# Row maxima of two heads exchanged in full on GpSimd, and one subtracting matrix product per segment part and head, in a causal block attention with a routed feed-forward

## The chip, the cores and the metric

The kernel runs on one core of one Trainium2 chip. The metric is device time in microseconds (us); the kernel before has a median of 488.1 us over 3 runs (486.54 to 491.87).

The engines are called as the profile calls them: PE is TensorE's matrix products and PEld its weight loads (they overlap), DVE is VectorE, ACT is ScalarE, POOL is GpSimd, SP is SyncE, which here only issues DMAs. "L573" is line 573 of the kernel.

## What is computed

q, k and v have shape (8, 8, 576, 64): batch, heads, sequence, head width. The attention is causal over blocks of 64 positions: a query sees its own block of keys and all blocks before it. The result, as 4608 rows of 512, goes through a mixture of eight experts in which each row goes through one of them.

```
scores = scale * np.matmul(q, k.transpose(0, 1, 3, 2))
mask = block_i >= block_j
scores = np.where(mask, scores, -1000000000.0)
scores = scores - np.max(scores, axis=-1, keepdims=True)
attn = np.exp(scores)
attn = attn / (np.sum(attn, axis=-1, keepdims=True) + 1e-09)
attn_out = np.matmul(attn, v)
...
h = np.maximum(x[b, s] @ w1[e], 0.0)
out[b, s] = p[e] * (h @ w2[e])
```

The change touches one step of the attention: the row maximum, and how it is subtracted from the scores before the exponential.

## The kernel before, in words

**Pairs of heads in a pipeline.** The work of the attention is cut into 32 pairs of heads (NPR). One turn of the main loop (L869) works on four pairs at once, each at another stage: pair `a` is loaded, transposed, and its maxima are begun; pair `c = a - 1` gets its scores and exponentials; pair `e = a - 2` is multiplied with v; pair `x = a - 3` is stored and transposed for the gate. The order of instructions on every engine is written out by hand (manual schedule), so each engine works its queue in program order.

**Maxima.** `top` (L507) makes scores with queries on the partitions, in three jobs that share one PSUM buffer (`ps_m`, one copy). Jobs 0 and 1 take the query blocks 4 to 7 and 0 to 1: a product covers two query blocks (128 queries on 128 partitions) for each head, so that after DVE's `reduce_max` (L535) the first 64 partitions of `mx` hold the even block and the last 64 the odd one, with the two heads beside each other in two columns. Job 2 (L526, L543) takes blocks 8, 3 and 2 with a stationary operand in which each half of the partitions belongs to one head; there the halves already hold one head each.

**Exchange before.** After job 1, two copies of 64 x 3 values (L538, on DVE; for pair 0 on ACT) bring into columns 6 to 8 of each half what the other half has of its head. Every block of 4 to 7, 0 and 1 is then found for one head in its own column and for the other in one of the columns 6 to 8. `PLACE` (L505) tells where a block stands.

**Shift.** `shift` (L545) makes on POOL, out of n columns of `mx`, n diagonal blocks of 64 x 64 (`diag`, in bf16; `negi` is minus the identity). It is called for slots 0 to 3 and 4 to 8 after job 1 (L1013 to L1014 for pair 1, L1047 to L1049 for the others, at the end of a turn) and for slots 9 to 11 after job 2 (L889 and L895, at the start of the next turn).

**Scores and the subtraction.** Scores are made transposed, keys on the partitions and queries along the row, in four segments (`SEGS`, L366) of six parts in all: 448 + 64, 256 + 192, 320 and 320 queries. `products` (L550) writes a part for both heads, in fp32. `less` (L558) then adds, with a stationary operand of ones and a moving operand of diagonal blocks, minus the maximum of each query. Blocks 2, 3 and 8 take one product a head (L573). Blocks 0, 1 and 4 to 7 take two for each head (L583), one for the own column and one for the exchanged columns, over every second block. Together these are 34 products a pair (14 of L573, 20 of L583), each with a weight load of the same ones. The two heads use the upper and the lower 64 rows of the array. `expo` (L590) is the exponential on ACT.

**Order around the change.** Within one turn the queues are as follows.

- POOL: `shift` of job 1 from the end of the turn before, then one DMA of feed-forward weights (L64, called at L1062; two of them in turns 4 and 6), then `shift` of job 2 (L895), the cast of the finished rows (L464), three small casts of keys and queries (L976, L978), and the zeroing of a corner of `prob` after each exponential (L598).
- DVE: the reductions of job 1 (L535), the two copies (L538), `norm` of the rows of pair `x` (L481, L482), the reductions of job 2 (L543), the casts of keys and queries (L928, L939), the reduction of job 0 (L535), the small `norm_last` (L489 to L492). In turns 9 to 13, 17 to 21 and 25 to 31 the steps of routing are put between them.
- PE: job 2 of `top` (L526), 8 transposes of pair `a` (L912), 4 transposes of pair `x` (L620) that read what `norm` wrote, single transposes (L631, L963), the products of segments 0 and 1 (L554), `less` for both (L573, L583), job 0 (L515), the outputs of blocks 8 and 6 to 7 (L606, L614), the products and `less` of segments 2 and 3, job 1, and the other outputs (L614).

Of the kernel before, what the change touches and what calls it, by code (L numbers as in the profile page):

```python
# [16 lines left out]
def kernel(  # L17
# [11 lines left out]
    nc = tc.nc  # L29
    F32 = mybir.dt.float32  # L30
    BF16 = mybir.dt.bfloat16
# [4 lines left out]
    ALU = mybir.AluOpType  # L36
# [3 lines left out]
    NB = S // block  # L40
# [5 lines left out]
    P = 128  # L46
# [40 lines left out]
    def rt(shape, dt, name):  # L87
        return rt_p.tile(shape, dt, tag=name, name=name)
# [5 lines left out]
    ones = rt([P, P], BF16, "ones")  # L94
# [37 lines left out]
    scr = rt([P, XGB * XW + XBB * Dm], BF16, "scr")  # L132
# [221 lines left out]
    def slots(inv, tok_g, tok_s):  # L354
# [4 lines left out]
        if tok_s is not None:  # L359
# [6 lines left out]
    SEGS = [[(1, 128, 448, 0), (4, 512, 64, 448)],  # L366
            [(0, 0, 256, 0), (3, 384, 192, 256)],
            [(2, 256, 320, 0)],
            [(0, 256, 320, 0)]]
# [32 lines left out]
    with tc.manual_schedule():  # L402
# [6 lines left out]
        def const(shape, dt, name):  # L409
            return cst.tile(shape, dt, tag=name, name=name)  # L410


        negi = const([P, 64], F32, "negi")
# [14 lines left out]
            nc.gpsimd.memset(vt[i][:, :, :, D:D + 1], 1.0)  # L428
            nc.gpsimd.memset(vt[i][64:128, 4], 0.0)

        diag0 = scr[:, 0:12 * 64].rearrange("p (s t) -> p s t", t=64)
        diag1 = const([P, 12, 64], BF16, "diag")
        nats, pls, mxs, xs, xbs, xTs = {}, {}, {}, {}, {}, {}

        def load_qk(i, engs=(nc.sync,)):
# [59 lines left out]
        def rows(h):  # L495
            return slice(64 * h, 64 * h + 64)
# [8 lines left out]
        PLACE = {4: 0, 6: 2, 0: 4, 2: 9, 3: 10, 8: 11}  # L505

        def top(i, job, pool):  # L507


            ps = pool.tile([P, 2, 512], F32, tag="s" if pool is ps_sp else "m", name="ps_m")  # L510
            flat = ps.rearrange("p b c -> p (b c)")
            if job < 2:
                for k, (b, c, n) in enumerate(PAIRS[job]):
                    for h in range(2):
                        nc.tensor.matmul(ps[:, h, c:c + n], lhsT=qh[rows(h), 64 * b:64 * b + 128],  # L515
                                         rhs=kh[rows(h), 0:n], start=(k == 0), stop=False)
                for h in range(2):
                    last = ps[:, h, :].rearrange("p (k t) -> p k t", t=64)[:, 5 if job else 7:8:2, :]
                    nc.tensor.matmul(last, lhsT=unseen[rows(h), :],  # L519
                                     rhs=ones[rows(h), :].rearrange("p (k t) -> p k t", t=64)  # L520
                                     [:, 0:2 if job else 1, :], start=False, stop=True)
                return ps
            for (b, c, n) in FULL:
                for (k0, nn) in ((0, min(n, 512)), (512, n - 512)):
                    if nn > 0:
                        nc.tensor.matmul(flat[:, c + k0:c + k0 + nn], lhsT=qd[:, PLACE[b] - 9, :],  # L526
                                         rhs=kh[:, k0:k0 + nn], start=True, stop=True)
            return ps

        def maxima(i, job, ps):  # L530
            flat = ps.rearrange("p b c -> p (b c)")
            mx = mxs[i]
            if job < 2:
                for (b, c, n) in PAIRS[job]:
                    nc.vector.reduce_max(mx[:, PLACE[b]:PLACE[b] + 2], ps[:, :, c:c + n], axis=AX)  # L535
                if job == 1:
                    for h in range(2):
                        (nc.vector.tensor_copy if i else nc.scalar.copy)(  # L538
                            mx[rows(h), 6:9], mx[rows(1 - h), h:6:2])
                return  # L540
            for (b, c, n) in FULL:
                z = PLACE[b]
                nc.vector.reduce_max(mx[:, z:z + 1], flat[:, c:c + n], axis=AX)  # L543

        def shift(i, s0, n):  # L545
            nc.gpsimd.tensor_tensor(  # L546
                (diag1 if i else diag0)[:, s0:s0 + n, :], negi[:, None, :].to_broadcast([P, n, 64]),
                mxs[i][:, s0:s0 + n, None].to_broadcast([P, n, 64]), op=ALU.mult)

        def products(i, ps, s, part):  # L550

            j, a, n, c = SEGS[s][part]
            for h in range(2):
                nc.tensor.matmul(ps[:, h, c:c + n],  # L554
                                 lhsT=pls[i][rows(h), S + 128 * j:S + 128 * j + 128],
                                 rhs=pls[i][rows(h), a:a + n], start=part == 0, stop=False)

        def less(i, ps, s, part):  # L558

            j, a, n, c = SEGS[s][part]  # L560
            diag = diag1 if i else diag0
            blocks = range(a // 64, (a + n) // 64)
            ends = part == len(SEGS[s]) - 1
            for b, w in ((0, 1), (2, 2), (4, 2), (8, 1)):
                if b not in blocks:
                    if b == 4 and 6 in blocks:
                        b, w = 6, 1
                    else:
                        continue
                o, z = c + 64 * b - a, PLACE[b]  # L570
                if b in (2, 8):
                    for h in range(2):
                        nc.tensor.matmul(ps[:, h, o:o + 64 * w], lhsT=ones[rows(h), :],  # L573
                                         rhs=diag[rows(h), z:z + w, :], start=False,
                                         stop=ends and b + w - 1 == blocks[-1])
                    continue
                for e in range(2):
                    for h in range(2):
                        out_s = ps[:, h, o:o + 128 * w].rearrange("p (m e t) -> p m e t", e=2, t=64)
                        zz = slice(z + h, z + h + 2 * w - 1, 2)  # L580
                        if e:
                            zz = slice(6 + z // 2, 6 + z // 2 + w)
                        nc.tensor.matmul(out_s[:, :, e ^ h, :], lhsT=ones[rows(h), :],  # L583
                                         rhs=diag[rows(h), zz, :], start=False,
                                         stop=ends and e == 1 and b + 2 * w - 1 == blocks[-1])

        def seg_tile():
            return ps_sp.tile([P, 2, 512], F32, tag="s", name="ps_s")
# [280 lines left out]
        for it in range(-2, NPR):  # L869
            a, c, e, x = it + 2, it + 1, it, it - 1  # L870
# [14 lines left out]
                last_ps = top(c, 2, ps_mp) if c > 1 else second  # L885
            if last_ps is not None and not on_a:
                maxima(c, 2, last_ps)
                shift(c, 9, 3)
            if on_x:  # L889
                norm(x, g0_b, 0, 6)  # L890
            run(it, "top")
            run(it, "begin", ge)
            if last_ps is not None and on_a:
                maxima(c, 2, last_ps)
                shift(c, 9, 3)  # L895
            if on_x:
                store_x(x, nc.gpsimd.tensor_copy if it < NPR - 1 else nc.scalar.copy)
            if it == NPR - 1:
# [2 lines left out]
            if on_a:  # L901
# [3 lines left out]
                else:  # L905
                    ps = ps_sp.tile([P, 2, 512], F32, tag="s", name="ps_t")
# [84 lines left out]
            if on_c:  # L991
                ps0, ps1 = seg_tile() if c else opened, seg_tile()
                if c:
                    products(c, ps0, 0, 0)
                products(c, ps1, 1, 0)
                products(c, ps1, 1, 1)
                if c:
                    products(c, ps0, 0, 1)
                else:
                    maxima(a, 0, top(a, 0, ps_mp))  # L1000
                if a in (1, 2):
                    g1 = turns()
                if a == 1:
                    load_weights(halves.pop(0))
                for z, ps in enumerate((ps0, ps1)):
                    less(c, ps, z, 0)
                    less(c, ps, z, 1)
                    expo(c, ps, z)
# [2 lines left out]

            if a == 1:
                maxima(a, 1, top(a, 1, ps_mp))  # L1013
                shift(a, 0, 4)  # L1014
                shift(a, 4, 5)
            elif on_a:
                maxima(a, 0, top(a, 0, ps_mp))
            if on_x and not on_a:
# [16 lines left out]
            if on_c:  # L1035
                pss = seg_tile(), seg_tile()
                products(c, pss[0], 2, 0)
                products(c, pss[1], 3, 0)
                if a == 1:
                    second = top(a, 2, ps_mp)  # L1040
                for z in range(2):
                    less(c, pss[z], z + 2, 0)
                    expo(c, pss[z], z + 2)
            run(it, "late", g1)
            if on_a:
                if a != 1:
                    maxima(a, 1, top(a, 1, ps_mp if a else ps_sp))  # L1047
                    shift(a, 0, 4)
                    shift(a, 4, 5)  # L1049
                if a == 0:  # L1050

                    opened = seg_tile()
                    products(a, opened, 0, 0)
                    products(a, opened, 0, 1)
                    maxima(a, 2, top(a, 2, ps_mp))
                    shift(a, 9, 3)
            if it >= 0:

                for _ in range(2 if it in (4, 6) else 1):
# [179 lines left out]
```

## Time and profile before

| what | value |
|---|---|
| median of the runs | 488.1 us (486.54 to 491.87, 3 runs) |
| profiled execution, device time | 487.98 us |
| its span, first to last instruction | 486.2 us |
| mean granted TensorE clock | 0.993 |
| instructions in the span | 19978 |
| POOL busy | 267.5 us (55%) |
| ACT busy | 252.3 us (52%) |
| HBM | 170 GB/s over the span |

The profile is of one execution. Its device time is 1.8 us longer than its span, and it lies 0.1 us below the median. A busy share is an average over all stages: the attention loop runs until about 335 us, the feed-forward after it. In the timeline, a row gives the start, the time from the first start to the last end of the instructions merged in it, engine, line, operation, tiles, count, and in brackets the idle time before it with what ended it.

### The profile page before, as it was taken

What the parts mean: (1) busy time and instruction counts of PE and PEld (TensorE: products, weight loads), DVE (VectorE), ACT (ScalarE), POOL (GpSimd) and SP (SyncE); (2) the same over time, 40 slices, a digit from 0 to 9 for tenths busy, and PEclk for the clock granted to TensorE, in tenths of its full rate; (3) what the DMA queues carried; (4) which work ended last, traced back from release to release, by engine and by line L of the source; (5) the groups of instructions that cost most, each with busy time, mean ns of one, the idle gap of its engine ahead of it and who ended that gap; (6) DMA issues with size and microseconds to landing.
All of it is one profiled execution on the core that took longest, in us unless ns stands there. A gap on an engine that the chain in (4) does not pass through costs nothing.

```text
span 486.2 us, 19978 instructions
## 1 busy us (share of the span) xinstructions
PE 469.7 (97%) x7959; PEld 374.7 (77%) x7980; DVE 343.4 (71%) x868; ACT 252.3 (52%) x512; POOL 267.5 (55%) x477
## 2 busy tenths in 40 slices
PE   8999999999999999999999999999999999999992
PEld 6687888888878888887888887878777777676770
DVE  5688767778898887889877879996468953434330
ACT  4645555455545455554555554544545545555551
POOL 3455444544445554444554345354587778888761
PEclk9999999999999999999999999999999999999997
DMA  7787999997999789787888878634556666667541
GB/s 153 137 179 135 167 171 185 187 158 148 172 165 157 149 156 170 147 162 145 138 164 161 166 142 165 104 60 100 122 152 149 132 151 164 145 150 150 149 115 50
DMA packets 180974, 71.33 MB, mean 147 GB/s; under 512 B 165008, under 2 KB 173200, under 8 KB 180880
## 3 DMA queue, kind: packets, MB, share of 16 engines
q1 hardware_dynamic: 161920, 37.93, 38.4%
q0 software_dynamic: 17760, 31.79, 35.1%
q8 instruction: 66, 1.08, 1.0%
q10 hardware_dynamic: 1200, 0.30, 0.3%
q14 instruction: 28, 0.23, 0.2%
HBM read 67.45 MB, written 14.97 MB: 170 GB/s over the span
## 4 chain that ended last, share of the span: by engine, by line
PE 86%; DVE 6%; DMA 2%; issue 2%; POOL 1%; ACT 1%; POOLq 0%; DVEq 0%; ACTq 0%
PE ps_s L554 18%; PE g L614 15%; PE ps_h L744 13%; PE ps_o L756 12%; PE ps_t L912 5%; PE g L606 4%; PE ps_m L526 3%; PE g L620 3%; PE ps_s L583 3%; PE ps_m L515 3%; DMA out_dram<-o_sb,tok2s 2%; DVE mx L535 2%; PE g L663 2%; PE ps_s L573 2%; DVE mx L543 1%
## 5 line engine op out<-in xcount | busy, mean ns | idle before, releaser
L593 ACT ACTIVATE prob<-ps_s 128x640 f32<-128x640 f32 (+2 forms) x128 | 100.2, 834 | 86.7 <-PE ps_s L573 62.7
L554 PE MATMUL ps_s<-plb 64*128 64x320 f32 (+4 forms) x768 | 105.9, 407 | 0.0
L535 DVE TENSOR_REDUCE mx<-ps_m 128x2 f32<-128x1024 f32 (+2 forms) x96 | 80.2, 864 | 32.3 <-PE ps_m L519 32.1
L546 POOL TENSOR_TENSOR diag<-negi,mx 128x256 bf16<-128x256 f32 (+2 forms) x93 | 59.5, 640 | 52.8 <-DVE mx L535 18.1
L614 PE MATMUL g<-vt,prob 128*64 128x65 f32 x2560 | 87.7, 223 | 0.2 <-issue 0.2
L554 PEld LDWEIGHTS ps_s<-plb 64*128 64x128 f32 x768 | 66.8, 186 | 24.8 <-issue 9.6
L598 POOL MEMSET prob<- 64x128 f32 x128 | 23.9, 200 | 108.5 <-ACT prob L593 108.5
L614 PEld LDWEIGHTS g<-vt,prob 128*64 128x64 f32 x2560 | 80.3, 138 | 3.7 <-issue 0.3
L756 PE MATMUL ps_o<-w_bf,hT 128*128 x283 | 67.4, 379 | 1.7 <-issue 0.7
L748 ACT ACTIVATE hT<-ps_h 128x512 bf16<-128x512 f32 x76 | 45.2, 597 | 19.8 <-PE ps_h L744 19.5
L924 ACT COPY plb<-ps_t 128x512 f32<-128x512 f32 x58 | 31.1, 589 | 42.5 <-PE ps_t L912 42.5
L760 ACT ACTIVATE o_sb<-ps_o,share 128x512 f32<-128x512 f32 x38 | 26.1, 687 | 45.8 <-PE ps_o L756 39.8
L756 PEld LDWEIGHTS <-hT 128*128 128x128 bf16 x304 | 28.3, 98 | 27.8
L543 DVE TENSOR_REDUCE mx<-ps_m 128x1 f32<-128x576 f32 (+2 forms) x96 | 43.0, 503 | 3.8 <-PE ps_m L526 3.6
L720 DVE COPY natb<-w_bf 128x4096 bf16 x20 | 24.6, 1228 | 29.9 <-PE ps_h L744 27.4
L720 DVE COPY plb<-w_bf 128x4096 bf16 x20 | 24.5, 1227 | 26.5 <-PE ps_h L744 25.3
L744 PEld LDWEIGHTS <-natb 128*128 128x128 bf16 x608 | 35.5, 98 | 4.6 <-issue 0.3
L744 PEld LDWEIGHTS <-plb 128*128 128x128 bf16 x608 | 35.5, 98 | 4.4 <-issue 0.3
L766 POOL DMA_INDIRECT out_dram<-o_sb,tok x20 | 30.3, 1517 | 13.2 <-ACT o_sb L760 8.2
L766 POOL DMA_INDIRECT out_dram<-o_sb,tok2s x18 | 30.7, 1704 | 11.6 <-ACTq L1191 4.8
L912 PE MATMUL ps_t<-id_f,natb 128*128 128x128 f32 x232 | 30.1, 273 | 0.0
L583 PEld LDWEIGHTS <-ones 64*128 64x128 bf16 x640 | 23.4, 94 | 7.8 <-issue 5.4
(271 smaller groups left out, 827.6 us busy)
## 6 DMA issues: line engine op xcount, KB each, us to landing
w_bf<-in_moe_w_dram POOLq DMA_DIRECT2D x32, 512.0 KB, 6.5
vt<-in_v_dram SPq DMA_DIRECT2D x64, 128.0 KB, 4.0
natb<-in_k_dram SPq DMA_DIRECT2D x63, 128.0 KB, 4.0
natb<-in_q_dram SPq DMA_DIRECT2D x63, 128.0 KB, 3.4
x_rows<-xb SPq DMA_DIRECT2D x32, 128.0 KB, 5.4
natb<-in_k_dram SPq DMA_DIRECT2D x32, 32.0 KB, 2.5
vt<-in_v_dram SPq DMA_DIRECT2D x32, 32.0 KB, 6.5
x_rows<-xb SPq DMA_DIRECT2D x64, 8.0 KB, 3.9
```

What stands on the lines that cost most here:

```text
L535: nc.vector.reduce_max(mx[:, PLACE[b]:PLACE[b] + 2], ps[:, :, c:c + n], axis=AX)
L543: nc.vector.reduce_max(mx[:, z:z + 1], flat[:, c:c + n], axis=AX)
L546: nc.gpsimd.tensor_tensor((diag1 if i else diag0)[:, s0:s0 + n, :], negi[:, None, :].to_broadcast([P, n, 64]), mxs[i][:, s0:s0 + n, None]. ...
L554: nc.tensor.matmul(ps[:, h, c:c + n], lhsT=pls[i][rows(h), S + 128 * j:S + 128 * j + 128], rhs=pls[i][rows(h), a:a + n], start=part == 0, ...
L593: nc.scalar.activation(p[:, :, SEG0[s]:SEG0[s] + w], ps[:, :, 0:w], func=AF.Exp, scale=scale_attn)
L614: nc.tensor.matmul(g[rows(e), o + 65 * h:o + 65 * h + 65], lhsT=p[:, h, c:c + 64], rhs=t[:, j, h, :], start=(j == 0), stop=(j == m))
L720: nc.vector.tensor_copy(w, w1_bf[:, bass.ds(off, WE)])
L744: nc.tensor.matmul(ps_h[:, f, :], lhsT=w[:, ko * F + fo * P:ko * F + fo * P + P], rhs=xb[:, ko * P:(ko + 1) * P], start=(ko == 0), stop=(k ...
L748: nc.scalar.activation(hT[:, half * 4:half * 4 + 4, :], ps_h, func=AF.Relu)
L756: nc.tensor.matmul(ps_o, lhsT=hT[:, fo, :], rhs=w2_bf[:, bass.ds(woff + fo * Dm, Dm)], start=(fo == 0), stop=(fo == FO - 1))
L766: wr = nc.gpsimd.indirect_dma_start(out=out_flat, out_offset=bass.IndirectOffsetOnAxis(ap=g[1][:, g[3]:g[3] + 1], axis=0), in_=o_sb, in_of ...
L912: tr = nc.tensor.transpose(pw[w][:, 128 * t:128 * t + 128], nat[:, 4 * w + t].rearrange("p h d -> p (h d)"), id_f)
```

## The change

The exchange becomes a full one. Three copies of 64 x 3 values, on POOL (for pair 0 on ACT), swap the odd columns of the first half with the even columns of the second, with columns 6 to 8 of the second half as the place in between. After that each half holds one head for all blocks. `shift` is now called by block instead of by slot, so `diag` has 9 blocks instead of 12 in the order of the queries: blocks 4 to 7 and then 0 to 1 after job 1, blocks 2 to 3 and then 8 after job 2. `less` is one product for each part and head, over all its blocks.

```
-        diag0 = scr[:, 0:12 * 64].rearrange("p (s t) -> p s t", t=64)
-        diag1 = const([P, 12, 64], BF16, "diag")
+        diag0 = scr[:, 0:NB * 64].rearrange("p (s t) -> p s t", t=64)
+        diag1 = const([P, NB, 64], BF16, "diag")
...
                 if job == 1:
-                    for h in range(2):
-                        (nc.vector.tensor_copy if i else nc.scalar.copy)(
-                            mx[rows(h), 6:9], mx[rows(1 - h), h:6:2])
+                    copy = nc.gpsimd.tensor_copy if i else nc.scalar.copy
+                    copy(mx[rows(1), 6:9], mx[rows(0), 1:6:2])
+                    copy(mx[rows(0), 1:6:2], mx[rows(1), 0:6:2])
+                    copy(mx[rows(1), 0:6:2], mx[rows(1), 6:9])
...
-        def shift(i, s0, n):
+        def shift(i, b, n):
+            z = PLACE[b]
             nc.gpsimd.tensor_tensor(
-                (diag1 if i else diag0)[:, s0:s0 + n, :], negi[:, None, :].to_broadcast([P, n, 64]),
-                mxs[i][:, s0:s0 + n, None].to_broadcast([P, n, 64]), op=ALU.mult)
+                (diag1 if i else diag0)[:, b:b + n, :], negi[:, None, :].to_broadcast([P, n, 64]),
+                mxs[i][:, z:z + n, None].to_broadcast([P, n, 64]), op=ALU.mult)
...
             j, a, n, c = SEGS[s][part]
             diag = diag1 if i else diag0
...
+            for h in range(2):
+                nc.tensor.matmul(ps[:, h, c:c + n], lhsT=ones[rows(h), :],
+                                 rhs=diag[rows(h), a // 64:(a + n) // 64, :], start=False,
+                                 stop=part == len(SEGS[s]) - 1)
...
                 maxima(c, 2, last_ps)
-                shift(c, 9, 3)
+                shift(c, 2, 2)
+                shift(c, 8, 1)
...
                 maxima(a, 1, top(a, 1, ps_mp))
-                shift(a, 0, 4)
-                shift(a, 4, 5)
+                shift(a, 4, 4)
+                shift(a, 0, 2)
```

The last two hunks stand for all places: `shift(c, 9, 3)` occurs in three places (L888, L895 and, for pair 0, L1056), the pair of `shift(a, 0, 4)` and `shift(a, 4, 5)` in two. The two branches of `less` by block are gone.

More of the change, by code (lines that the diff above doesn't have):

```diff
@@ L561, in less @@
             diag = diag1 if i else diag0
[L562 to L585, printed above, removed]
+            for h in range(2):
+                nc.tensor.matmul(ps[:, h, c:c + n], lhsT=ones[rows(h), :],
+                                 rhs=diag[rows(h), a // 64:(a + n) // 64, :], start=False,
+                                 stop=part == len(SEGS[s]) - 1)
         def seg_tile():
@@ L894 @@
                 maxima(c, 2, last_ps)
-                shift(c, 9, 3)
+                shift(c, 2, 2)
+                shift(c, 8, 1)
             if on_x:
@@ L1047 @@
                     maxima(a, 1, top(a, 1, ps_mp if a else ps_sp))
-                    shift(a, 0, 4)
-                    shift(a, 4, 5)
+                    shift(a, 4, 4)
+                    shift(a, 0, 2)
                 if a == 0:
@@ L1055 @@
                     maxima(a, 2, top(a, 2, ps_mp))
-                    shift(a, 9, 3)
+                    shift(a, 2, 2)
+                    shift(a, 8, 1)
             if it >= 0:
```

## Prediction

> **What bounds the kernel now.** I read the totals and the chain of work that ended last first, to learn which engine a saving must come from; then one plain turn in order of time; then the waits of PE.
>
> ```profile
> PE 469.7 (97%) x7959; PEld 374.7 (77%) x7980; DVE 343.4 (71%) x868; ACT 252.3 (52%) x512; POOL 267.5 (55%) x477
> ...
> PE 86%; DVE 6%; DMA 2%; issue 2%; POOL 1%; ACT 1%; POOLq 0%; DVEq 0%; ACTq 0%
> ```
>
> PE carries 86% of the chain, DVE 6%, POOL 1%. A busy PE counts pipelined products at full latency, so 97% isn't yet "at its peak"; what matters is the step from one start to the next. The chain shows these steps, in a plain turn (168.2 to 178.0 us):
>
> ```profile
> 172.49 0.06 PE ps_s L573 x2
> ...
> 172.92 0.22 PE ps_m L515 x2
> ...
> 176.11 0.11 PE ps_s L583 x4
> ...
> 176.39 0.22 PE ps_m L515 x4
> ```
>
> The 22 products of `less` for segments 0 and 1 occupy PE from 172.49 to 172.92, 0.43 us; the 12 for segments 2 and 3 from 176.11 to 176.39, 0.28 us. L515 streams 512 columns a head in 0.22 us, both heads at once: 0.43 ns a column. `less` moves 960 columns a head in the first group and 640 in the second, at that rate 0.41 and 0.27 us. So the small products already run at the speed of their columns.
>
> The same turn in order of time shows who waits:
>
> ```profile
> 167.82 0.58 PE L614 MATMUL g<-vt,prob 128*64 128x65 f32 x14
> ...
> 167.99 0.61 POOL L546 TENSOR_TENSOR diag<-negi,mx 128x256 bf16<-128x256 f32 x1 [0.50 <-DVE mx L535]
> ...
> 168.21 0.59 DVE L538 COPY mx<-mx 64x3 f32<-64x3 f32 x2
> ...
> 168.78 1.04 PE L912 MATMUL ps_t<-id_f,natb 128*128 128x128 f32 x8
> 168.83 0.20 DVE L481 RECIPROCAL rs<-g 128x6 f32<-128x6 f32 x1
> 168.95 0.72 POOL L546 TENSOR_TENSOR diag<-negi,mx 128x320 bf16<-128x320 f32 x1 [0.34 <-PE ps_m L526]
> 169.06 0.56 DVE L482 TENSOR_TENSOR x<-g,rs 128x384 f32<-128x384 f32 x1
> ...
> 169.54 1.34 DVE L543 TENSOR_REDUCE mx<-ps_m 128x1 f32<-128x576 f32 x3
> 169.61 0.74 POOL L64 DMA_DIRECT2D w_bf<-in_moe_w_dram  x1
> ...
> 169.77 0.63 PE L620 MATMUL g<-id_f,x 128*128 128x128 f32 x4
> ...
> 170.80 0.42 DVE L928 CAST kh<-plb 128x512 bf16<-128x512 f32 x1
> ...
> 171.04 0.54 POOL L546 TENSOR_TENSOR diag<-negi,mx 128x192 bf16<-128x192 f32 x1 [0.69 <-DMA vt<-in_v_dram]
> ...
> 172.33 0.22 PE L573 MATMUL ps_s<-diag,ones 64*128 64x128 bf16 x2
> ```
>
> Read it from the copies. DVE ends them at 168.80 and only then begins `norm` (168.83 to 169.62). PE's transposes L620 read `norm`'s result and begin at 169.77. POOL's last diagonal blocks are ready at 171.58, `less` needs them at 172.33: 0.75 us of room. POOL is idle between 170.35 and 171.04, because it waits for DVE's L543 (ends 170.88). In a turn where `norm` was early, the same two PE rows are:
>
> ```profile
> 66.16 1.04 PE L912 MATMUL ps_t<-id_f,natb 128*128 128x128 f32 x8
> ...
> 67.03 0.60 PE L620 MATMUL g<-id_f,x 128*128 128x128 f32 x4
> ```
>
> From the first L912 to the first L620 there it is 0.87 us, in the plain turn 0.99, and L620 itself takes 0.63 instead of 0.60. So PE loses 0.15 us a plain turn behind DVE's copies. The view of waits counts such turns:
>
> ```profile
> PEld g L620 <- issue: 2.3, 14, 0.2
> ...
> PE ps_m L526 <- DVE mx L535: 1.6, 3, 0.6
> ```
>
> The first row is the gap ahead of L620, 14 times. The second is three turns in which routing fills DVE and PE waits over half a microsecond for the reductions of job 1; there DVE is the chain for a whole turn.
>
> **The change part by part.**
>
> *Products of `less`.* 34 become 12 a pair, 1088 become 384, with as many fewer weight loads; the columns stay the same. Gain: 0.43 - 0.41 and 0.28 - 0.27, 0.03 us a pair, over 32 pairs 0.9 us. Bounds: nothing, and twice that from the rounding of the chain's rows. I take 0.9.
>
> The Trainium skill ("TensorE: Matmul & The Clock Gate", Back-to-back issue gap) gives a sustained pace of about 81 ns a product at 128 columns, set by product and weight load together. Thirty-four of them at that pace would be 2.8 us a pair, where this trace has 0.71; the measurement decides, and the rule's direction (many small products are dear) is the first rival.
>
> *Copies off DVE.* `norm` can then start when PE's outputs are there. L614 of the turn before ends at 168.40; the shortest step from such an output to a DVE reader is read here:
>
> ```profile
> 173.73 1.10 PE L614 MATMUL g<-vt,prob 128*64 128x65 f32 x32
> ...
> 174.95 0.18 DVE L489 RECIPROCAL rs<-g 128x3 f32<-128x3 f32 x1 [0.52 <-PE g L614]
> ```
>
> It is 0.12 us, so `norm` starts at 168.52 instead of 168.83, 0.31 us earlier, and ends at 169.31. That is before PE comes to L620 (169.65), so the whole 0.15 us go, 14 times: 2.1 us. What is late next is PE itself. In the three DVE-bound turns the same 0.31 us come off the wait of 0.55: 0.9 us in all. Bounds of these two together: nothing (another wait takes over), and 2.1 + 1.6 = 3.7. I take 3.0.
>
> *Three copies onto POOL.* No row shows a POOL copy of 64 x 3. The nearest are small and simple:
>
> ```profile
> L598 POOL MEMSET prob<- 64x128 f32 x128 | 23.9, 200 | 108.5 <-ACT prob L593 108.5
> ...
> L976 POOL CAST kh<-plb 128x64 bf16<-128x64 f32 x32 | 7.6, 238 | 7.2 <-ACT plb L974 7.2
> ...
> L538 DVE COPY mx<-mx 64x3 f32<-64x3 f32 x62 | 18.1, 291 | 1.5
> ```
>
> Below, 0.20 each, 0.6 for three back to back. Each copy reads or overwrites what the one before touched, on other partitions, so it may wait for its end. For a step between two dependent POOL instructions I have only the start of the kernel, where the identity is set to zero and then filled:
>
> ```profile
> 0.81 0.20 POOL masks.py:197 MEMSET id_f<- 128x128 f32 x1 [0.29 <-POOLq L1223]
> ...
> 1.16 0.28 POOL masks.py:199 TENSOR_SCALAR_AFFINE_SELECT id_f<-id_f 128x128 f32<-128x128 f32 x1
> ```
>
> From end to start 0.15. Above, DVE's mean of 0.29 plus 0.15, three times: 1.33 us. I take 0.9, three times 0.2 plus two waits of 0.15, as a copy of 3 columns is nearer to the small rows.
>
> The Trainium skill ("GPSIMD Engine Reference", Instruction dispatch) states that consecutive Pool instructions are no barrier between its cores and that a reader of another core's partitions needs a wait; this speaks for the waits in that sum, and no row here shows these copies.
>
> *Shift.* By the rows of L546 256 elements take 0.61, 320 take 0.72, 192 take 0.54: some 0.1 for each 64. So 128 take 0.41 and 64 take 0.30 (estimates). After job 1, 0.61 + 0.72 become 0.61 + 0.41; after job 2, 0.54 becomes 0.71 in two instructions. POOL's queue in the plain turn is then: reductions end 168.17, first copy 168.33 (DVE to POOL is 0.16 at 170.88 to 171.04), copies to 169.23, blocks 4 to 7 to 169.84, 0 to 1 to 170.25, weight DMA to 170.99. DVE's L543 now ends at 170.57, so POOL is no longer idle but the later one: blocks 2 to 3 and 8 are ready at 171.70. `less`, 0.15 earlier, needs them by 172.18 - 0.05. Hidden, with 0.43 us of room instead of 0.75. Behind POOL's queue stand the cast L464, its DMAs on SP, and L976 and L978, all 0.1 to 0.2 later; their readers are the next turn's loads and job 2, microseconds away. If the cover goes, PE waits directly (rival three).
>
> DVE's casts run just then and can hold POOL up. One such row:
>
> ```profile
> 202.38 1.02 POOL L546 TENSOR_TENSOR diag<-negi,mx 128x192 bf16<-128x192 f32 x1 [0.94 <-DMA vt<-in_v_dram]
> ```
>
> 1.02 instead of 0.54: 0.48 lost. With one such loss the blocks are ready at 172.18, 0.05 too late; I count that at nothing here.
>
> *Where POOL isn't hidden: the last pair.* At 322.9 there is no next pair and nothing between job 2 and `less`:
>
> ```profile
> 322.96 0.59 DVE L538 COPY mx<-mx 64x3 f32<-64x3 f32 x2
> ...
> 323.70 0.72 POOL L546 TENSOR_TENSOR diag<-negi,mx 128x320 bf16<-128x320 f32 x1 [0.34 <-PE ps_m L526]
> ...
> 324.36 0.79 POOL L64 DMA_DIRECT2D w_bf<-in_moe_w_dram  x1
> ...
> 325.24 0.49 POOL L546 TENSOR_TENSOR diag<-negi,mx 128x192 bf16<-128x192 f32 x1
> ...
> 325.79 0.23 PE L573 MATMUL ps_s<-diag,ones 64*128 64x128 bf16 x2 [0.22 <-POOL diag L546]
> ```
>
> Here PE waits for POOL already. New: copies from 323.09 to 323.99, shifts to 325.01, DMA to 325.80, two shifts to 326.51, `less` at 326.56: 0.8 us later. Turns 4 and 6 have a second weight DMA of 0.74 ahead of the shift and may lose 0.1 each.
>
> *Pair 0.* ACT makes three copies instead of two, ahead of a cast that is on the chain:
>
> ```profile
> 10.05 0.40 ACT L538 COPY mx<-mx 64x3 f32<-64x3 f32 x2 [2.03 <-DVE mx L535]
> ...
> 10.47 0.59 ACT L932 CAST kh<-g 128x512 bf16<-128x512 f32 x1
> ```
>
> 0.20 more.
>
> *Sum.* -0.9 - 3.0 + 0.8 + 0.2 + 0.2 = -2.7 us. The profiled execution took 487.98 us, so 485.3; it stands 0.1 below the median of the runs, which I leave out.
>
> **The rivals.**
>
> *Weight loads were the price.* The loads of ones are busy for 45.9 us:
>
> ```profile
> L573 PEld LDWEIGHTS <-ones 64*128 64x128 bf16 x448 | 22.5, 102 | 0.6 <-issue 0.3
> ...
> L583 PEld LDWEIGHTS <-ones 64*128 64x128 bf16 x640 | 23.4, 94 | 7.8 <-issue 5.4
> ```
>
> Were PE held by them, 704 of 1088 gone would be 29.7 us: 458. Against it: 22 products in 0.43 us, 20 ns each, while a load takes 94; they overlap. Chance 0.04.
>
> *The wait moves and nothing is gained.* L620 no longer waits, but PE then waits elsewhere for as long (for DVE's casts, for ACT), and the three DVE-bound turns stay. Left are -0.9 + 1.2: 488.3. Against it: PE's waits within the loop in the view of waits are these two rows and gaps of 0.1 to 0.2 that recur whoever was last. Chance 0.18.
>
> *Slower: POOL's chain outlasts its room in every turn.* Place: the product of blocks 8 in front of `less`. Copies at 1.33 us end at 169.66, the weight DMA at 171.42, the two shifts at 172.13, with one loss of 0.48 at 172.61; `less` begins at 172.66, 0.33 later than before, in some 28 turns: +9.2; gains of `norm` are then worth nothing, `less` gives 0.9, last pair (0.4 dearer), turns 4 and 6 and pair 0 cost 1.6. Sum 488.0 + 9.9 = 497.9. It decides from 172.28 on (before's start less 0.05), and passes 1% at 0.18 us a turn more. For it: POOL's reserve shrinks in any case. Against: before, POOL lost its 0.48 in only a few turns. Chance 0.14.
>
> The Trainium skill ("SBUF — State Buffer", SBUF: two separate sides) says that GpSimd and a DVE instruction in a two-port mode take a shared port as an exclusive lock for a whole instruction. The 1.02 above agrees with it; two shifts in place of one could be held twice.
>
> **How the numbers follow.** Forecast 485.3 with a chance of 0.64, its own range 483.4 (both waits gone, `less` at twice its gain, copies at 0.6: -4.6) to 487.5 (half of the 3.0 lost, and POOL 0.05 too late in 14 turns: +2.2). The rivals have 0.04, 0.18 and 0.14. The range, 482.3 to 491.0, takes in the second rival and the mild part of the third, and leaves out the first and most of the third; below, it goes 1.1 further than the forecast's own, since the runs of before alone differ by more (486.54 to 491.87). About 1%, 4.9 us, is what a measurement of this kernel can tell from no change: faster than 483.1 has 0.04 from the first rival and 0.06 from the forecast's tail; slower than 493.0 has 0.12 from the third; within has 0.78.
>
> **What would show it.** Right: 12 rows of `less` a pair, the chain's steps at 0.41 and 0.27 us; L481 about 0.3 us after the reductions' end instead of behind copies; the row of L620's gap gone; L526's wait for L535 at about 0.2 us; POOL's wait for L543 gone in plain turns. Wrong: a row in which PE waits for L546 in more than a handful of turns (third rival); L554 or L515 with new waits of 0.15 (second); `less` far below 0.41 us (first).

## The result, and the profile after

The changed kernel takes 484.87 us (median of 7 runs, 484.32 to 485.98). Its ratio to the kernel before is 0.9924, with a 95% interval of 0.9896 to 0.9953: 0.8% faster. Its profiled execution took 484.87 us, with a span of 483.2. The forecast was 485.3.

The totals and the chain of work that ended last:

```profile
PE 468.3 (97%) x7276; PEld 369.1 (76%) x7276; DVE 327.1 (68%) x806; ACT 252.4 (52%) x513; POOL 271.6 (56%) x602
...
PE 75%; POOL 9%; issue 7%; DMA 4%; DVE 2%; POOLq 1%; ACT 0%; DVEq 0%
```

PE has 683 products fewer on record and yet only 1.4 us less busy time. DVE lost 16 us. The chain's share of POOL (9%, it was 1%) comes from the gathers of the feed-forward, not from the attention: within the loop the chain runs almost wholly over PE, from turn to turn. In its steps, in a plain turn:

```profile
170.50 0.41 PE ps_s L568 x8
170.91 0.22 PE ps_m L515 x2
...
174.10 0.27 PE ps_s L568 x4
174.37 0.22 PE ps_m L515 x4
```

`less` is L568 now. Eight products take 0.41 us where 22 took 0.43, four take 0.27 where twelve took 0.28. The same turn in order of time:

```profile
166.39 0.18 POOL L540 COPY mx<-mx 64x3 f32<-64x3 f32 x1 [0.74 <-DVE mx L535]
...
166.60 0.20 DVE L481 RECIPROCAL rs<-g 128x6 f32<-128x6 f32 x1 [0.27 <-PE g L599]
166.64 0.18 POOL L541 COPY mx<-mx 64x3 f32<-64x3 f32 x1
...
166.83 0.56 DVE L482 TENSOR_TENSOR x<-g,rs 128x384 f32<-128x384 f32 x1
...
166.88 0.18 POOL L542 COPY mx<-mx 64x3 f32<-64x3 f32 x1
166.93 1.04 PE L899 MATMUL ps_t<-id_f,natb 128*128 128x128 f32 x8
167.15 0.97 POOL L551 TENSOR_TENSOR diag<-negi,mx 128x256 bf16<-128x256 f32 x2
...
167.81 0.60 PE L605 MATMUL g<-id_f,x 128*128 128x128 f32 x4
168.06 0.74 POOL L64 DMA_DIRECT2D w_bf<-in_moe_w_dram  x1
...
168.82 0.89 POOL L551 TENSOR_TENSOR diag<-negi,mx 128x128 bf16<-128x128 f32 x2
...
170.33 0.58 PE L568 MATMUL ps_s<-diag,ones 64*128 64x448 bf16 x8
```

DVE's `norm` (L481) now waits for PE's outputs, 0.27 us after the reductions, and no longer stands behind copies. It ends at 167.39, and PE goes from the transposes L899 to L605 in 0.88 us (166.93 to 167.81) without a gap; L605 takes 0.60 instead of 0.63. POOL's last blocks are ready at 169.71, 0.62 us ahead of `less`.

In the routing turns that DVE set, PE now starts L526 nearly in step:

```profile
134.63 1.28 DVE L535 TENSOR_REDUCE mx<-ps_m 128x2 f32<-128x768 f32 x2
...
135.95 0.20 DVE L481 RECIPROCAL rs<-g 128x6 f32<-128x6 f32 x1
...
136.05 0.60 PE L526 MATMUL ps_m<-kh,qd 128*128 128x512 bf16 x4 [0.15 <-PE g L599]
```

Its gap was 0.55 and is 0.15. DVE still sets these turns: L526 starts 0.14 us after the reductions L535 end (135.91), as it did before (0.15). Measured from one start of L526 to the next, by the chain and the timeline, the turns are as follows; turns in which `norm` was early anyway are mostly 0.03 shorter.

| turn | before | after |
|---|---|---|
| plain (45.02 to 54.84; 45.59 to 55.23) | 9.82 | 9.64 |
| set by DVE (209.58 to 219.93; 207.33 to 217.17) | 10.35 | 9.84 |

From the second start of L526 to the last the loop shrank from 307.67 us (15.41 to 323.08) to 302.72 (16.37 to 319.09), by 4.95. The span shrank by 3.0; the difference was lost at both ends.

At the start, the inputs of this execution came later, which the change doesn't touch: DVE's first reduction begins at 8.28, before at 7.59. What is the change's own is the third copy on ACT:

```profile
10.73 0.19 ACT L540 COPY mx<-mx 64x3 f32<-64x3 f32 x1 [1.61 <-DVE mx L535]
10.96 0.19 ACT L541 COPY mx<-mx 64x3 f32<-64x3 f32 x1
11.19 0.19 ACT L542 COPY mx<-mx 64x3 f32<-64x3 f32 x1
...
11.40 0.58 ACT L919 CAST kh<-g 128x512 bf16<-128x512 f32 x1
```

The cast on the chain starts 0.67 after the first copy; before it was 0.42 (10.05 to 10.47). At the end, the last pair:

```profile
319.00 0.18 POOL L540 COPY mx<-mx 64x3 f32<-64x3 f32 x1 [0.74 <-DVE mx L535]
...
319.75 0.97 POOL L551 TENSOR_TENSOR diag<-negi,mx 128x256 bf16<-128x256 f32 x2
...
320.67 0.79 POOL L64 DMA_DIRECT2D w_bf<-in_moe_w_dram  x1
...
321.48 0.81 POOL L551 TENSOR_TENSOR diag<-negi,mx 128x128 bf16<-128x128 f32 x2
...
322.35 0.59 PE L568 MATMUL ps_s<-diag,ones 64*128 64x448 bf16 x8 [0.77 <-POOL diag L551]
```

From the last start of L526 (319.09) to `less` it is 3.26 us; before it was 2.71 (323.08 to 325.79). PE waits 0.77 for POOL there, and this is the only wait of PE for L551 in the loop.

### The profile page after: what moved, and what is told of

The parts are those of the page before. It is cut to its first block, busy times and chain, and to the rows that moved or that the text cites. A ratio compares the mean times of both kernels' runs of the same rounds, so it can differ in the third digit from the quotient of the medians.

```text
span 483.2 us, 18592 instructions
## 1 busy us (share of the span) xinstructions
PE 468.3 (97%) x7276; PEld 369.1 (76%) x7276; DVE 327.1 (68%) x806; ACT 252.4 (52%) x513; POOL 271.6 (56%) x602
## 4 chain that ended last, share of the span: by engine, by line
PE 75%; POOL 9%; issue 7%; DMA 4%; DVE 2%; POOLq 1%; ACT 0%; DVEq 0%
PE ps_s L559 20%; PE g L599 16%; PE ps_t L899 5%; PE ps_h L729 5%; PE ps_o L741 5%; PE g L591 5%; PE ps_s L568 5%; POOL scr L689 4%; PE ps_m L526 3%; POOL xg L689 3%; PE ps_m L515 3%; PE g L605 3%; DMA out_dram<-o_sb,tok2s 2%; POOL out_dram L751 2%; PE g L648 2%
## 5 line engine op out<-in xcount | busy, mean ns | idle before, releaser
L535 DVE TENSOR_REDUCE mx<-ps_m 128x2 f32<-128x1024 f32 (+2 forms) x96 | 80.3, 864 | 35.4 <-PE ps_m L519 33.8
L599 PEld LDWEIGHTS g<-vt,prob 128*64 128x64 f32 x2560 | 80.1, 138 | 3.3
L741 PE MATMUL ps_o<-w_bf,hT 128*128 x304 | 71.5, 379 | 0.1
L551 POOL TENSOR_TENSOR diag<-negi,mx 128x256 bf16<-128x256 f32 (+1 forms) x124 | 58.6, 491 | 9.9 <-DVE mx L546 5.2
L751 POOL DMA_INDIRECT out_dram<-o_sb,tok x20 | 24.6, 1232 | 16.1 <-ACT o_sb L745 12.6
L568 PE MATMUL ps_s<-diag,ones 64*128 64x448 bf16 (+1 forms) x372 | 31.5, 274 | 0.8 <-POOL diag L551 0.8
L899 PE MATMUL ps_t<-id_f,natb 128*128 128x128 f32 x232 | 30.1, 273 | 0.0
L591 PEld LDWEIGHTS g<-vt,prob 128*64 128x64 f32 x640 | 21.3, 137 | 7.2 <-issue 6.2
```

Source lines behind the costliest of these rows:

```text
L551: nc.gpsimd.tensor_tensor((diag1 if i else diag0)[:, b:b + n, :], negi[:, None, :].to_broadcast([P, n, 64]), mxs[i][:, z:z + n, None].to_b ...
L568: nc.tensor.matmul(ps[:, h, c:c + n], lhsT=ones[rows(h), :], rhs=diag[rows(h), a // 64:(a + n) // 64, :], start=False, stop=part == len(SE ...
L591: nc.tensor.matmul(g[rows(h), 130:195], lhsT=p[:, h, c:c + 64], rhs=t[:, j, h, :], start=(j == 0), stop=(j == 4))
L599: nc.tensor.matmul(g[rows(e), o + 65 * h:o + 65 * h + 65], lhsT=p[:, h, c:c + 64], rhs=t[:, j, h, :], start=(j == 0), stop=(j == m))
L741: nc.tensor.matmul(ps_o, lhsT=hT[:, fo, :], rhs=w2_bf[:, bass.ds(woff + fo * Dm, Dm)], start=(fo == 0), stop=(fo == FO - 1))
L899: tr = nc.tensor.transpose(pw[w][:, 128 * t:128 * t + 128], nat[:, 4 * w + t].rearrange("p h d -> p (h d)"), id_f)
```

## The experiments

The theory: the gain is the copies' time off DVE's queue, which lets `norm` start earlier; the products give only their 0.03 us a pair; POOL takes the copies for nothing because it has room. The rivals: the fewer products and weight loads are the gain; or POOL is already what a turn waits for.

The experiments ran in three sessions, each on a chip of its own: e1 to e4 in the first, e5_act_last_dma, e6 and e7 in the second, the runs named "again" and e8 in the third. There the kernel before takes 498.2 to 498.7 us, and single runs spread over several us. In the changed kernel the difference lies behind the loop: from the last start of L526 to the end it takes 175.0 us in the third session and 164.1 in the result. So totals are given as ratios to the kernel before in the same session, and the verdicts rest on the turns of the loop, which repeat to 0.01 us where nothing disturbs them (9.64 for a plain turn of the changed kernel, there and in the result).

**The changed kernel again** (a0_after_again, no edit).

> The changed kernel again, unedited, beside the edits below on one chip. If the gain is the loop's 0.17 a plain turn and 0.5 in three turns, the ratio to the kernel before is again 0.992 to 0.995, whatever the chip's own time is.

Ratio 0.9945 (0.9908 to 0.9982), as expected. Plain turns 9.64, DVE's turns 9.85.

**Old exchange, its two copies on POOL** (e1_pool_copies).

```
-                        (nc.vector.tensor_copy if i else nc.scalar.copy)(
+                        (nc.gpsimd.tensor_copy if i else nc.scalar.copy)(
```

> The kernel before with one edit: the two copies of the old exchange run on GpSimd instead of VectorE; the 34 products of less stay. Theory (the gain comes from taking the copies off VectorE's queue ahead of norm): the gap ahead of L620 goes and the three VectorE-bound turns get 0.5 shorter, so 485.5, 0.8 above the changed kernel, which is what the products give. Rival (the gain is the fewer products and weight loads): 487.5 to 488.5.

```profile
44.46 0.61 PE L526 MATMUL ps_m<-kh,qd 128*128 128x512 bf16 x4
...
54.13 0.61 PE L526 MATMUL ps_m<-kh,qd 128*128 128x512 bf16 x4
```

A plain turn takes 9.67 us: of the 0.18 that the change gives, 0.15 come with this edit alone, with all 34 products still there. The turns set by DVE take 9.95 instead of 10.35. The total doesn't follow: ratio 0.9986 (0.9960 to 1.0013), where 485.5 of 488.1, so 0.995, was expected; it lies where the rival had it. The turns speak against the rival, since the gain in them is there without fewer products. Its profile, of an execution of 500.5 us where the median is 497.7, shows where time went instead, in stretches where PE waits for nothing that the profile shows:

```profile
PE g L614 <- issue: 2.1, 3, 1.3
PE ps_s L554 <- issue: 2.0, 1, 2.0
```

Over the loop its turns are some 7 us longer than others of their kind. In the changed kernel's first profile this view has one such stretch in the loop, of 0.2. More of this below.

**Full exchange, on DVE** (e2_exchange_dve).

```
-                    copy = nc.gpsimd.tensor_copy if i else nc.scalar.copy
+                    copy = nc.vector.tensor_copy if i else nc.scalar.copy
```

> The changed kernel with the full exchange on VectorE: three copies instead of two ahead of norm, 12 products a pair. Theory: VectorE's copies take 0.6 to 0.9 a turn where they took 0.59, norm starts 0 to 0.3 later than in the kernel before, less gives 0.8: 487.2 to 491. Rival (fewer products and weight loads are the gain): 484.9, as the changed kernel.

```profile
45.78 0.54 PE ps_m L526 x4
...
55.53 0.54 PE ps_m L526 x4
```

A plain turn takes 9.75 to 9.76, DVE's turns 10.21; ratio 0.9995 (0.9970 to 1.0019). With the 12 products but the exchange on DVE, most of the gain is gone. By their turns, the rival of the products falls on this and the run before. In the totals neither half of the change alone can be told from the kernel before (0.9986 and 0.9995), and only both together can. DVE's copies were cheaper than I had allowed:

```profile
167.85 0.16 DVE L540 COPY mx<-mx 64x3 f32<-64x3 f32 x1
...
168.24 0.17 DVE L542 COPY mx<-mx 64x3 f32<-64x3 f32 x1
...
168.44 0.20 DVE L481 RECIPROCAL rs<-g 128x6 f32<-128x6 f32 x1
```

Three take 0.16 each. Of the two of before the first took 0.42 and the second 0.16, in nearly every turn: the first ran beside POOL's shift and ended with it (168.63, the shift at 168.60), the second came after it. Now POOL waits for the copies.

**One product for each block** (e3_less_by_block, and again as e3_again).

```
-            for h in range(2):
-                nc.tensor.matmul(ps[:, h, c:c + n], lhsT=ones[rows(h), :],
-                                 rhs=diag[rows(h), a // 64:(a + n) // 64, :], start=False,
-                                 stop=part == len(SEGS[s]) - 1)
+            for b in range(a // 64, (a + n) // 64):
+                o = c + 64 * b - a
+                for h in range(2):
+                    nc.tensor.matmul(ps[:, h, o:o + 64], lhsT=ones[rows(h), :],
+                                     rhs=diag[rows(h), b, :], start=False,
+                                     stop=part == len(SEGS[s]) - 1 and 64 * b + 64 == a + n)
```

> The changed kernel with less cut into one product for each block of 64 queries and head: 50 products and weight loads a pair instead of 12, the same columns. Theory (columns set the time, some 2 ns more for each pair of products): 44 ns a pair of heads, 1.4 us in all: 486.3, and the chain's rows of less at about 0.46 and 0.29 us. Rival (a weight load costs the 42 ns of the rival's price): 1216 more loads, 51 us, about 536.

> 50 products a pair again, beside the changed kernel. Theory of the columns alone: 1.4 us above the changed kernel. Rival (TensorE also stands without a wait shown when its instruction stream is longer, 7 us in the first profile of this kernel, 0.2 in the changed one): 4 to 8 us above it.

```profile
39.70 0.44 PE ps_s L570 x30
40.13 0.22 PE ps_m L515 x2
...
43.32 0.29 PE ps_s L570 x20
43.61 0.22 PE ps_m L515 x4
```

Fifty products take 0.44 and 0.29 us where twelve take 0.41 and 0.27; a plain turn is 9.69, 0.05 longer. So 38 more products with their weight loads cost 0.05 us, about 1.3 ns each, and the price of 42 ns is refuted. But the totals rise by more than the 1.4 us that this makes over 27 turns: ratios 1.0020 (0.9989 to 1.0050) and 1.0036 (1.0002 to 1.0069), the second beside 0.9945 for the changed kernel in the same session, 4.5 us by the ratios. In the second profile the loop is 306.47 us against 302.34: 1.4 from the products, and the rest from a few turns that are 0.4 to 0.8 too long. One of them in the chain:

```profile
84.97 0.56 issue
85.53 0.34 PE g L601 x4
```

PE stands in the middle of a run of equal products. The kernel before stands in the same turn, four products before the same L526, and once more two turns later:

```profile
85.29 0.17 issue
...
105.51 0.29 issue
```

The changed kernel doesn't there, in any session. It stands at another place, ahead of the gate's products (L648) in the turn that starts at 136 us in the result, which is 0.25 longer than its kind there. PE stands at the same place with one more POOL instruction (e6), with the last DMA moved (e8) and with the copies on ACT as well (e5_again), all with 12 products:

```profile
148.12 0.43 PE L648 MATMUL g<-xT,wgl 128*32 128x128 f32 x8 [1.23 <-issue]
146.70 0.43 PE L648 MATMUL g<-xT,wgl 128*32 128x128 f32 x8 [0.88 <-issue]
146.58 0.43 PE L648 MATMUL g<-xT,wgl 128*32 128x128 f32 x8 [0.60 <-issue]
```

The traces show what these places have in common. The thirteen profiles have 27 such stands of over 0.15 us in the loop. If PE's products and weight loads are counted from the start of the trace, each stand comes after a number of them that leaves 193 when it is divided by 256, so the stands of a trace lie whole blocks of 256 instructions apart. And each time a packet of 16384 bytes in the queue that loads instructions had landed 1.3 to 1.7 us before PE went on. So PE stood at the end of a block when the packet had come late. That the packet holds the next instructions, and is the cause, is read from these counts and times; no run delayed or hastened one.

This is the rival of the second expectation, though in less than its first profile (about 7 us of such stretches) had shown. A longer stream passes its blocks faster: in the loop one lasts 6.7 us before, 7.3 in the changed kernel and 6.4 here (medians), and the queue has 66, 61 and 70 packets. What the stands cost varies between executions: by the turns beyond the length of their kind, 0.8 and 0.4 us in the two profiles of the changed kernel, 1.3 before and some 7 in e1 with 34 products, 3 and 9 with 50.

**Copies on ACT in all turns** (e4_act_copies).

```
-                    copy = nc.gpsimd.tensor_copy if i else nc.scalar.copy
+                    copy = nc.scalar.copy
```

> The changed kernel with the three copies on ScalarE for all pairs. ScalarE is idle for 1.6 us at this place in a plain turn. Theory (it matters only that VectorE is relieved): the same time as the changed kernel, 484.9, within 0.5. Rival (GpSimd's chain is what the turn waits for): 0.5 or more faster, since GpSimd's queue is 0.55 shorter in busy time.

Ratio 0.9976 (0.9941 to 1.0011), which overlaps the changed kernel's of another session. Plain turns 9.64, DVE's 9.85, the same to 0.01. Two turns of its profile are 1.2 us longer: there DVE waits for POOL's cast L464, which waits 5.0 us for the DMA of the rows before. The profile of e5_act_last_dma has three such turns, that of e5_again, also with the copies on ACT, none; whether the copies on ACT have a part in it stays open. By the undisturbed turns, it matters that DVE is relieved, not by whom.

**POOL made later** (e6_pool_1 and e7_pool_3): one or three more instructions of 128 elements ahead of `shift` of job 2.

```
             if last_ps is not None and on_a:
+                for _ in range(1):
+                    nc.gpsimd.tensor_tensor(
+                        diag1[:, 2:4, :], negi[:, None, :].to_broadcast([P, 2, 64]),
+                        negi[:, 0:2, None].to_broadcast([P, 2, 64]), op=ALU.mult)
                 maxima(c, 2, last_ps)
                 shift(c, 2, 2)
```

> The changed kernel with one more GpSimd instruction of 128 elements (about 0.4 us; its result is overwritten) ahead of the shift of job 2, in every turn but the last pair's. Theory (GpSimd has 0.57 of room in a plain turn): nearly hidden, 485.3, at most 0.5 more than the changed kernel. Rival (GpSimd sets the turn already): 0.4 in 29 turns, 12 us, 496.5.

> The same with three such instructions, 1.2 us. Theory: the room of 0.57 is used up and the rest shows, 0.7 in some 17 plain turns, 0.8 in three, 0.3 in four, 1.1 in one: about 16 us, 501, with TensorE waiting for L551 in most turns. If the room is larger than I read: less than 5 us.

One such instruction is hidden in the plain turns: they stay at 9.64. Three turns are 0.19 longer, three 0.15 and one 0.4, together 1.4 us, and the stand shown above adds to them, where at most 0.5 was expected; the ratio is 0.9955 (0.9925 to 0.9984). Three are not hidden: ratio 1.0280 (1.0215 to 1.0345), as expected, plain turns 10.41 to 10.46, and PE waits where the slower rival had placed it:

```profile
PE ps_s L568 <- POOL diag L551: 15.5, 23, 1.2
```

So the room is there and is between 0.4 and 1.2 us. In the plain turn at 165.6 us POOL's last blocks come 1.33 us later after L526 than in the changed kernel and the turn is 0.77 longer, so some 0.56 was room and the rest shows. The rival had the right place and the wrong size.

**The last weight DMA behind the last shift** (e8_last_dma; e5_act_last_dma and e5_again have the copies on ACT as well).

```
             if last_ps is not None and not on_a:
                 maxima(c, 2, last_ps)
                 shift(c, 2, 2)
                 shift(c, 8, 1)
+                load_weights(halves.pop(0))
...
-                for _ in range(2 if it in (4, 6) else 1):
+                for _ in range(2 if it in (4, 6) else 0 if it == NPR - 3 else 1):
```

> The changed kernel with one edit: the last weight DMA is issued behind the shift of the last pair. Theory: TensorE's wait of 0.77 for L551 in the last pair falls below 0.1, and the time falls by 0.5 to 0.8. Rival (the rows of the feed-forward arrive by DMA at their own time, and PE waits 1.3 for them there in the changed kernel): PE's wait goes, the time stays within 0.3.

> As the kernel with the copies on ScalarE, and the last weight DMA is issued behind the shift of the last pair instead of ahead of it. Theory (in the last pair TensorE waits 0.77 for GpSimd, and the DMA holds its queue for 0.79): that wait goes, 0.5 to 0.8 less than without the move: 484.2. If the end of the attention is set by something else: no change.

> Copies on ScalarE and the last weight DMA moved, again, beside the changed kernel. Theory: equal to the kernel with the DMA alone moved, within 0.3 per mille, since GpSimd is not waited for in the loop.

```profile
PE ps_s L568 <- POOL diag L551: 0.3, 1, 0.3
```

PE's wait in the last pair falls from 0.8 to 0.3 in all three runs, where it was expected to go or to fall below 0.1. The ratios are 0.9945 (0.9914 to 0.9976) for the move alone, 0.9950 (0.9916 to 0.9984) and 0.9939 (0.9913 to 0.9964) with ACT, beside 0.9945 for the changed kernel: no difference that these runs could tell, and half a microsecond is below what they tell. Whether it is lost at the next wait stays open; in the changed kernel such a wait exists, a few us later, for rows that arrive by DMA:

```profile
338.56 1.61 PE L729 MATMUL ps_h<-scr,plb 128*128 128x128 bf16 x26 [1.30 <-DMA scr<-scr]
```

No version was shown to be faster than the changed kernel.

## Why the prediction was right, step by step

- *Products of `less`*: 0.9 forecast. The turns that change in nothing else are 0.03 shorter; over the 27 turns that DVE doesn't set, 0.8. Right, and for the reason given: with the same columns, 50 products took 0.73 us and 12 took 0.68.
- *Copies off DVE*: 3.0 forecast. The gap ahead of the transposes is gone in the 14 turns that had it, 0.15 each, 2.1. The three turns set by DVE gave 0.5 each, 1.5 instead of 0.9, and this term was mis-sized in two ways. First, `norm` starts 0.39 earlier where I took 0.31: it waits for PE's outputs as I had said, but begins 0.05 after their end and not 0.12. The old exchange on POOL (e1) gives this part alone, 0.40. Second, the cast of the queries on DVE takes 0.1 less beside the shift by blocks, which I hadn't foreseen. In the same turn, before and after:

```profile
210.00 0.20 DVE L481 RECIPROCAL rs<-g 128x6 f32<-128x6 f32 x1
212.51 0.73 DVE L928 CAST qh<-plb 128x512 bf16<-128x512 f32 x1
...
207.35 0.20 DVE L481 RECIPROCAL rs<-g 128x6 f32<-128x6 f32 x1 [0.27 <-PE g L599]
209.86 0.63 DVE L915 CAST qh<-plb 128x512 bf16<-128x512 f32 x1
```

This second part isn't the copies' doing: the kernel with the full exchange on DVE (e2) has it too, and the one with the old shift (e1) hasn't. `less` has no share in these turns: with 50 products they are as long as with 12, to 0.01.
- *Copies on POOL*: 0.9 us assumed. By the rows above they start 0.25 apart and the shift follows 0.76 after the first start. Between the two bounds, and hidden, as forecast; room 0.62 where I had 0.43. The third rival's price, `less` 0.33 later than before, needed blocks about 1 us later than they came.
- *Last pair*: 0.8 forecast, 0.55 measured, for the same reason. *Pair 0*: 0.2 forecast, 0.25 measured. *Turns 4 and 6*: 0.2 forecast, nothing measured; both have the length of their kind.
- *Sum of the change's own terms*: -0.8 - 3.3 - 0.3 (the casts) + 0.55 + 0.25 = -3.6, against -2.7 forecast. The span fell by 3.0. The later inputs (+0.7), a feed-forward that took 0.5 longer in this execution (148.6 us from its first product to the end), and the stretches without a wait (some 0.6 less than before) make up the rest. That total and forecast lie 0.4 apart is thus partly luck: the change's own terms gave 0.9 more than I forecast, and what I hadn't in the sum (+0.7, +0.5, -0.6) took 0.6 back.
- *The first two rivals*: refuted by the block-wise products (0.05 us for 38 of them) and by the loop, in which L620's gap went without another taking its place.
- What I didn't foresee is that PE can stand at the end of a block of instructions, and that the length of the stream has a price through it.

## What to carry to other kernels

Before many small products are merged, read the step from start to start: here products in opposite halves of the array that reload the same weights cost little more than their columns, and merging them gave almost nothing. An instruction of half a microsecond on an engine that isn't the bound can still be what the bound waits for, if it comes in that engine's queue ahead of the one result that the bound reads; move it to a queue that has room there, and measure the room by adding work to it. Take a turn at a time where single runs spread by more than the effect: the turns repeat to 0.01 us. Where PE stands without a wait, count its instructions from one such stand to the next: a multiple of 256 pointed here at their loading.

## What the runs showed of the hardware

- A GpSimd copy of 64 x 3 values took 0.18 us, and three that depend on each other started 0.25 apart.
- A VectorE copy of 64 x 3 values took 0.42 us while GpSimd worked on the shift beside it, and 0.16 when GpSimd was idle. This agrees with the lock on the shared port in the Trainium skill ("SBUF — State Buffer", SBUF: two separate sides); no run here separates that lock from other reasons.
- TensorE can stand for 0.2 to 2 us with no wait that the profile shows. In the loop all 27 such stands of the thirteen profiles lay whole blocks of 256 products and weight loads apart, and ended 1.3 to 1.7 us after a packet of 16384 bytes landed in the instruction queue. The kernels with 34 and 50 products a pair stood in the same two turns, in four profiles out of four; with 12 products a pair these turns had no stand, and other places had.
